# Two sequence mixers in one kernel: the swapped copy of k made by an engine, the skip on TensorE, another load for x, and a new order

## The chip, the cores and the metric

One Trainium2 chip, one core of it. The metric is the device time of one execution in microseconds; less is better. The kernel before has a median of 215.62 us over three runs (215.46 to 218.27).

## The reference

Two mixers over a sequence of 2048 positions and 640 channels are computed and laid side by side. All data is bf16.

```python
# A: a diagonal complex state space model, 640 states
Lam_bar = exp(dt * Lam);  B_bar = ((Lam_bar - 1) / Lam)[:, None] * Bmat
h[t] = Lam_bar * h[t-1] + B_bar @ x[t]
a = 2 * Re(h @ Cmat.T) + x * Dskip
# B: a long convolution with two gates
kv = shift4(k, shift_k) * v          # a causal filter of 4 taps in each channel
y  = irfft(rfft(pad(kv)) * rfft(pad(ssm_k)))[:2048] + kv * ssm_D
b  = q * y
out = concatenate([a, b], axis=-1)   # 2048 x 1280
```

## The kernel before, in words

Everything is straight-line code. A plan lists some 500 items (`make_plan`), each with a name, the engine, its dependencies and a function; the string `ORDER` lists the names in the order in which they are recorded, so each engine's own order is that order restricted to its items. `@2` gives the PSUM pair that an item uses (four pairs, @0 to @6), and `!` picks the other engine for items that name one (an evacuation goes to VectorE instead of ScalarE). Instructions on one engine run in that order; waits between engines come from the data.

Mixer A treats the sequence in four phases s (position modulo 4), 512 positions each, and five blocks j of 128 states. x of phase s, channels on the partitions, is `xT{s}`: for the phases in `NAT` it is loaded naturally (`load_xn`), transposed by TensorE (`xt`) and copied out of PSUM (`xe`); for the others it is loaded by a transposing DMA on SyncE's queue (`load_xt`). Item `v{s}_{j}` (TensorE, `pe_in`) multiplies B and x, and for s other than 1 adds the previous phase times Lambda; `ve{s}_{j}` evacuates. The order in a block is s = 1, 2, 3, 0: phase 0 then holds four steps in one, and a scan over 512 positions is done on it: a rotation with a cosine and sine table (`tabs`, from POOL's phases `tp{j}` and ScalarE's `tab{j}`), the scan and the rotation back (`rs{j}`, `rout{j}`). `od{s}_{j}` makes the other phases from it on VectorE, and `p{i}_{s}` (TensorE, `pe_proj`) projects 128 positions of a phase onto the 640 outputs: 20 matmuls of 320 columns. The skip x * Dskip is added by six more matmuls with a diagonal matrix, or, for the eight blocks in `SKV`, by VectorE: x rows are loaded (`xs`), multiplied by Dskip (`skip_x`, `xd`) and added while evacuating (`dve_yo`). Otherwise ScalarE evacuates (`act_yo`). `yd{i}_{s}` stores.

Mixer B goes through five groups G of 128 channels. k and v are loaded transposed (`kT`, `vT`). The four taps (`tap{G}_{m}`) are matmuls of 64 x 64 diagonal matrices, two halves of the array at once, and need a second copy of k with its channel halves swapped, `kS`: two DMAs from SBUF to SBUF (`swap_k`). `kv` multiplies by v on VectorE, `kvo` stores kv to a DRAM scratch, `kvs` reads it back as rows, `hs` reads the filter. The transform is done in two steps of matmuls (`s1`, `s2`, h for the filter, k for kv; `he`/`ke` are the evacuations) with tables G and R, `y{G}_{hf}` is the complex product of the spectra on VectorE, `inv` the first inverse step with table H, `zt` a transposing DMA, `fin` the last step, `ob` the gate by q on VectorE, `od_` the store. The tables come from phases on POOL (`gp`, `hp`) through sines on ScalarE (`G`, `H`).

Of the kernel before, what the change touches and what calls it, by code (L numbers as in the profile page):

```python
# [29 lines left out]
SKV = [(i, s) for i in (2, 3) for s in range(4)]  # L30
RAW = (0, 1)
NAT = (1, 2)
# [13 lines left out]
class Kernel:  # L46
# [487 lines left out]
    def rotate(self, out, v, j, back):  # L534
        tt = self.nc.vector.tensor_tensor
        c, s = (self.tabs[:, j, i:i + 1, :].to_broadcast([128, 2, M]) for i in range(2))
        tt(out=self.rot_p, in0=c, in1=v, op=ALU.mult)  # L537
# [67 lines left out]
    def swap_k(self, eng):  # L605
        for h in range(2):
# [3 lines left out]
            eng.dma_start(out=self.kS[64 * h:64 * h + 64], in_=src)  # L610
# [56 lines left out]
    def dve_y(self, hf):  # L667
# [3 lines left out]
        cr = self.rot[:].rearrange("p a n -> p (a n)").rearrange("p (r n) -> p r n", r=2)  # L671
        tt(out=cr, in0=X[:, ::-1, :], in1=self.Hf[:, 1:2, hs].to_broadcast([128, 2, 1024]), op=ALU.mult)  # L672
        tt(out=X, in0=X, in1=self.Hf[:, 0:1, hs].to_broadcast([128, 2, 1024]), op=ALU.mult)  # L673
        for r in range(2):
            tt(out=X[:, r, :], in0=X[:, r, :], in1=cr[:, r, :], op=ALU.add if r else ALU.subtract)  # L675
# [39 lines left out]
def make_plan(K):  # L715
# [48 lines left out]
    for q in range(3):  # L764
        A(f"dL{q}", "DVE", 0.83, ["lam", "dc"], lambda q=q: K.dve_diagL(q))
# [58 lines left out]
    for j in J:  # L824
# [31 lines left out]
    for G in range(NG):  # L856
# [3 lines left out]
        dma(f"kS{G}", "SP", 1.1, 1.1, [f"kT{G}"] + ([f"tap{G - 1}_{m}" for m in range(2)] if pre else []), lambda e, G=G: K.swap_k(e))  # L860
# [51 lines left out]
s1h0_1@4 bg3@0 H2 s1h0_0@6 dS1 v3_0@2 gp2 H3 bge3!@0 s1he0_1@4 s1he0_0!@6 kT1 s1h0_2@0 ve3_0@2 s1h0_3@4 gp3 s1he0_2!@0 s1he0_3@4
nH kvs0 v0_0@6 G2 pow G3 s2h0_3@2 ve0_0!@6 s2h0_2@0 prr s2he0_3@2 s2h0_1@4 kS1 rs0 v1_4@6 s2he0_1@4 vT1 s2he0_2@0 ve1_4@6
s1k0_3@2 s1k0_0@4 s1ke0_3@2 s1k0_1@0 hs1 s1ke0_1!@0 tap1_0@6 s1k0_2@2 s1ke0_0!@4 tap1_1@0 s1ke0_2@2 s2h0_0@4 kv1_0@6 s2k0_1@2
s2he0_0@4 kv1_1@0 v1_2@6 s2ke0_1@2 rout0 kvo1 CT0 s2k0_2@4 ve1_2@6 s2k0_3@0 od2_0 s2k0_0@2 s2ke0_2@4 v1_1@6 s2ke0_3@0 kT2 had1
y0_1 s1h1_2@4 v2_2@0 s1he1_2@4 s2ke0_0@2 kvs1 ve1_1@6 s1h1_0@4 ve2_2@0 y0_0 s1h1_1@2 inv0_2@6 v3_2@0 zs0_2@6 s1he1_1@2 s1he1_0@4
# [92 lines left out]
```

## Time and profile before

| | |
|---|---|
| median of three runs | 215.62 us |
| the profiled execution | 216.61 us, of which the span is 214.8 |
| TensorE (PE) busy | 189.7 us, 88% |
| VectorE (DVE) busy | 187.6 us, 87% |
| ScalarE (ACT) busy | 130.4 us, 61% |
| POOL busy | 40.1 us, 19%, all in the first 44 us |
| DMA queue of SyncE | 86.6% of the 16 DMA engines' span |
| mean granted clock of TensorE | 0.984 |

A timeline row reads: start in us, duration in us, engine, line of the program, operation, output<-input, count, and in brackets the idle time before it and what ended that. A windows row reads: the window and its length, then busy time and number of instructions of PE, PEld (weight loads), DVE, ACT and POOL (or of the one engine or line that the question was confined to), then the granted clock, the DMA share and the GB/s. A group's row reads: line, engine, operation, tiles, shape, count | busy, mean ns | idle time before it.

### The profile page before, as it was taken

To read this page: it belongs to the slowest core of one execution; us is meant where nothing else is said; L and a number is where in the kernel's file an instruction comes from. 1 tells how busy PE (TensorE), PEld (TensorE's weight loads), DVE (VectorE), ACT (ScalarE), POOL (GpSimd) and SP (SyncE) were. 2 spreads that over 40 slices of the span, in tenths; PEclk is the share of its full clock that TensorE was granted. 3 is DMA by queue.
4 is the path that set the end of the run, shared out by engine and by line. 5 is a ranking of instruction groups with operands and counts; after the bars stand their busy time and mean duration, and the time that the engine had idled before them with its cause. 6 is when DMAs were issued, how large, how long until landed. Compare 5 with 4: busy or idle time off the path is not lost.

```text
span 214.8 us, 7500 instructions
## 1 busy us (share of the span) xinstructions
PE 189.7 (88%) x3322; PEld 129.3 (60%) x3322; DVE 187.6 (87%) x304; ACT 130.4 (61%) x145; POOL 40.1 (19%) x73
## 2 busy tenths in 40 slices
PE   0854849898999999899899999997999999999993
PEld 0723715455646647556775455775778787887772
DVE  2799899759999899999999999999999999991472
ACT  2392853877678586997977858785557856010100
POOL 8799999910000000000000000000000000000000
PEclk9998888999999999999999999999999999999999
DMA  6899902999699999899957999899880757888965
GB/s 185 216 248 183 184 5 79 191 174 176 158 219 148 159 194 148 156 168 197 164 142 155 140 198 157 139 242 197 193 139 3 160 165 167 125 205 167 206 199 145
DMA packets 123517, 35.41 MB, mean 165 GB/s; under 512 B 116055, under 2 KB 122844, under 8 KB 123484
## 3 DMA queue, kind: packets, MB, share of 16 engines
q1 hardware_dynamic: 123424, 34.92, 86.6%
q8 instruction: 26, 0.43, 0.9%
q14 instruction: 7, 0.06, 0.1%
q10 hardware_dynamic: 60, 0.01, 0.0%
HBM read 12.30 MB, written 7.86 MB: 94 GB/s over the span
## 4 chain that ended last, share of the span: by engine, by line
PE 51%; DVE 22%; POOL 10%; DMA 8%; ACT 4%; issue 3%; ACTq 1%; SPq 0%; DVEq 0%
PE ps L572 21%; PE ps L523 11%; PE ps L662 4%; DVE vT L638 4%; PE ps L649 4%; DMA zz<-zz 3%; DMA xT<-in_A_x_dram 3%; POOL qb L460 3%; POOL kv_st L460 2%; PE ps L683 2%; DMA As_h<-in_A_Lambda_im_dram 2%; PE ps L702 2%; DVE z L546 2%; DVE rot L537 1%; PE ps L684 1%
## 5 line engine op out<-in xcount | busy, mean ns | idle before, releaser
L523 PE MATMUL ps<-xT,BT 128*128 128x512 bf16 x200 | 51.6, 395 | 4.3 <-ACT xT L470 2.6
L523 PEld LDWEIGHTS <-BT 128*128 128x128 bf16 x200 | 19.1, 100 | 27.3 <-issue 6.1
L572 PE MATMUL ps<-Cs,hs 128*128 128x320 bf16 x240 | 34.9, 299 | 0.0
L572 PEld LDWEIGHTS <-hs 128*128 128x128 bf16 x240 | 22.5, 98 | 8.4
L662 PEld LDWEIGHTS <-G 128*64 128x64 bf16 x640 | 19.3, 109 | 7.3 <-issue 5.9
L470 ACT CAST Hf<-ps 128x1024 bf16<-128x1024 f32 x20 | 19.8, 1025 | 3.0 <-PE ps L662 3.0
L470 ACT CAST As_h<-ps 128x1024 bf16<-128x1024 f32 x17 | 16.7, 1027 | 7.0 <-PE ps L649 4.3
L470 ACT CAST zz<-ps 128x1024 bf16<-128x1024 f32 x15 | 14.6, 1030 | 7.7 <-PE ps L686 7.7
L470 ACT CAST Xs<-ps 128x1024 bf16<-128x1024 f32 x19 | 19.0, 1030 | 0.1
L470 ACT CAST As_kv<-ps 128x1024 bf16<-128x1024 f32 x17 | 16.9, 1027 | 2.9 <-PE ps L649 2.9
L683 PE MATMUL ps<-Xs,H 128*128 128x128 bf16 x80 | 17.6, 220 | 0.3 <-ACT Xs L470 0.2
L686 PE MATMUL ps<-Xs,H 128*128 128x128 bf16 x80 | 17.5, 219 | 0.0
L685 PE MATMUL ps<-Xs,H 128*128 128x128 bf16 x80 | 17.5, 219 | 0.0
L684 PE MATMUL ps<-Xs,H 128*128 128x128 bf16 x80 | 17.5, 219 | 0.0
L594 ACT CAST BT<-ps 128x640 bf16<-128x640 f32 x8 | 5.6, 695 | 18.2 <-PE ps L577 16.2
L633 PE MATMUL ps<-kT,diagS 64*64 64x512 bf16 x80 | 11.1, 397 | 5.1 <-DVE BT L468 2.8
L675 DVE TENSOR_TENSOR Xs<-Xs,rot 128x1024 bf16<-128x1024 bf16 x20 | 12.9, 687 | 0.3
L662 PE MATMUL ps<-As_kv,G 128*64 128x128 bf16 x320 | 11.7, 221 | 1.3 <-ACT As_h L470 1.2
L672 DVE TENSOR_TENSOR rot<-Xs,Hf 128x2048 bf16<-128x2048 bf16 x10 | 12.2, 1224 | 0.7
L662 PE MATMUL ps<-As_h,G 128*64 128x128 bf16 x320 | 12.1, 221 | 0.8 <-ACT zz L470 0.5
L673 DVE TENSOR_TENSOR Xs<-Xs,Hf 128x2048 bf16<-128x2048 bf16 x10 | 12.2, 1225 | 0.6
L470 ACT CAST hs<-ps 128x1024 bf16<-128x1024 f32 x8 | 8.2, 1020 | 6.4 <-PE ps L526 5.2
(201 smaller groups left out, 422.4 us busy)
## 6 DMA issues: line engine op xcount, KB each, us to landing
h_st<-in_B_ssm_k_dram SPq DMA_DIRECT2D x10, 256.0 KB, 5.7
kv_rows<-vT SPq DMA_DIRECT2D x5, 512.0 KB, 3.3
kv_st<-kv_rows SPq DMA_DIRECT2D x10, 256.0 KB, 5.5
qb<-in_B_q_dram SPq DMA_DIRECT2D x5, 512.0 KB, 5.7
out_dram<-qb SPq DMA_DIRECT2D x5, 512.0 KB, 3.9
out_dram<-BT SPq DMA_DIRECT2D x16, 160.0 KB, 2.8
kS<-kT SPq DMA_DIRECT2D x10, 129.0 KB, 3.3
zz<-in_A_x_dram SPq DMA_DIRECT2D x2, 640.0 KB, 4.2
```

The costliest lines, as they stand in the source:

```text
L470: self.nc.scalar.copy(out=out, in_=in_)
L523: mm(o, lhsT=self.BT[:, r, k, j * 128:(j + 1) * 128], rhs=xT[:, k, :], start=(k == 0), stop=(s == 1 and k == NT - 1))
L572: mm(o[:, 0:320], lhsT=h[:, r, ts], rhs=self.Cs[:, r, j, c0:c0 + 320], start=(j == 0 and r == 0), stop=(not on_pe and j == NT - 1 and r == 1))
L633: self.nc.tensor.matmul(ps[cols, r, :], lhsT=self.diagS[rows, 4 * v + j, :], rhs=rhs, start=(j == 0), stop=(j == 3))
L662: self.nc.tensor.matmul(o[64 * e:64 * e + 64, c:c + 128], lhsT=self.G[:, r, k, :], rhs=As[:, k, :], start=True, stop=True)
L672: tt(out=cr, in0=X[:, ::-1, :], in1=self.Hf[:, 1:2, hs].to_broadcast([128, 2, 1024]), op=ALU.mult)
L673: tt(out=X, in0=X, in1=self.Hf[:, 0:1, hs].to_broadcast([128, 2, 1024]), op=ALU.mult)
L675: tt(out=X[:, r, :], in0=X[:, r, :], in1=cr[:, r, :], op=ALU.add if r else ALU.subtract)
L683: mm(o_re, lhsT=self.H[:, 0, k1, :], rhs=yre, start=True, stop=False)
L684: mm(o_re, lhsT=self.H[:, 2, k1, :], rhs=yim, start=False, stop=True)
L685: mm(o_im, lhsT=self.H[:, 1, k1, :], rhs=yre, start=True, stop=False)
L686: mm(o_im, lhsT=self.H[:, 0, k1, :], rhs=yim, start=False, stop=True)
```

## The change

- `swap_k` becomes an item of VectorE, or of ScalarE where the order marks it with `!`: two copies of 64 partitions x 1032 elements from one partition half to the other, in place of the two DMAs. In the new order kS0 stays on VectorE and kS1 to kS4 are marked.
- `SKV` is empty: all sixteen projection blocks add the skip on TensorE and are evacuated by ScalarE. The x rows, their multiplication and their sum on VectorE go.
- `NAT` is (1,): x of phase 2 is loaded by a transposing DMA; its 20 transposes on TensorE and two evacuations go.
- The VectorE items are cut: rs into rs, sc; rout into ra, rout; od into oa, od; y into ya, y. The instructions in them are the same.
- `ORDER` is another.

```diff
-SKV = [(i, s) for i in (2, 3) for s in range(4)]
+SKV = []
-NAT = (1, 2)
+NAT = (1,)
...
-    def swap_k(self, eng):
+    def swap_k(self):
         for h in range(2):
             o = PAD - 4 + 512 * h
             src = self.kT[64 - 64 * h:128 - 64 * h, o:o + 1024 + 516]
             src = bass.AP(src.tensor, src.offset, [list(src.ap[0]), [1024, 2], [1, 516]])
-            eng.dma_start(out=self.kS[64 * h:64 * h + 64], in_=src)
+            if self.alt:
+                self.nc.scalar.copy(out=self.kS[64 * h:64 * h + 64], in_=src)
+            else:
+                self.nc.vector.tensor_copy(out=self.kS[64 * h:64 * h + 64], in_=src)
...
-        A(f"rs{j}", "DVE", 4.3, [f"ve0_{j}", f"tab{j}", "prr"], lambda j=j: K.dve_scan(j))
-        A(f"rout{j}", "DVE", 2.05, [f"rs{j}"], lambda j=j: K.dve_out(j))
+        A(f"rs{j}", "DVE", 2.05, [f"ve0_{j}", f"tab{j}"], lambda j=j: K.dve_rot(j))
+        A(f"sc{j}", "DVE", 2.25, [f"rs{j}", "prr"], lambda j=j: K.dve_scan(j))
+        A(f"ra{j}", "DVE", 1.25, [f"sc{j}"], lambda j=j: K.dve_back(j))
+        A(f"rout{j}", "DVE", 0.8, [f"ra{j}"], lambda j=j: K.dve_out(j))
         for s in (1, 2, 3):
-            A(f"od{s}_{j}", "DVE", 2.26, [f"rout{j}", "pow"], lambda j=j, s=s: K.dve_next(j, s))
+            A(f"oa{s}_{j}", "DVE", 0.9, [f"rout{j}", "pow"], lambda j=j, s=s: K.dve_mul(j, s))
+            A(f"od{s}_{j}", "DVE", 1.36, [f"oa{s}_{j}"], lambda j=j, s=s: K.dve_next(j, s))
...
-        dma(f"kS{G}", "SP", 1.1, 1.1, [f"kT{G}"] + ([f"tap{G - 1}_{m}" for m in range(2)] if pre else []), lambda e, G=G: K.swap_k(e))
+        A(f"kS{G}", "DVE", 0.7, [f"kT{G}"] + ([f"tap{G - 1}_{m}" for m in range(2)] if pre else []), lambda: K.swap_k(), alt=("ACT", 2.0))
...
         for hf in range(2):
-            A(f"y{G}_{hf}", "DVE", 3.73, [f"s2ke{G}_{q}" for q in (2 * hf, 2 * hf + 1)] + [f"s2he{G}_{q}" for q in (2 * hf, 2 * hf + 1)],
-              lambda hf=hf: K.dve_y(hf))
+            A(f"ya{G}_{hf}", "DVE", 2.4, [f"s2ke{G}_{q}" for q in (2 * hf, 2 * hf + 1)] + [f"s2he{G}_{q}" for q in (2 * hf, 2 * hf + 1)],
+              lambda hf=hf: K.dve_ym(hf))
+            A(f"y{G}_{hf}", "DVE", 1.33, [f"ya{G}_{hf}"], lambda hf=hf: K.dve_y(hf))
...
-x1 pc lv2 lv0 B0 lv3 pc2 dc3 lsk lv4 dc lv1 pg dc2 gp1 zer kT0 tv@0 pc3 tsk@2 tve@0 B4 exp gp0 B3 rho Fi bt0@4 rr x2 B1 tske@2
+x1 pc lv1 lv4 B1 lv0 pc2 dc lv2 zer lv3 B0 lsk pc3 dc3 kT0 dsel pg pk dc2 gp1 tv@0 tsk@2 tve@0 den exp gp0 rho bt1@4 tske@2 rr
...
```

What the new order moves is seen in the instructions. SyncE's queue in the start, before: from the natural load of x2 (into zz) to the second k.

```order
L179 DMA zz_162<-in_A_x_dram 128x4x640
L176 DMA As_kv_160<-in_A_B_re_dram 128x640
L176 DMA As_kv_160<-in_A_B_im_dram 128x640
L603 DMA_TRANSPOSE vT_155<-in_B_v_dram 128x2048
L610 DMA kS_154<-kT_153 64x2x516 x2
L614 DMA h_st_156<-in_B_ssm_k_dram 64x32x64 x2
L176 DMA As_kv_160<-in_A_B_re_dram 128x640
L176 DMA As_kv_160<-in_A_B_im_dram 128x640
L182 DMA_TRANSPOSE xT3_138<-in_A_x_dram 128x5x512
L641 DMA kv_rows_63<-vT_155 128x2048
L182 DMA_TRANSPOSE xT0_135<-in_A_x_dram 128x5x512
L603 DMA_TRANSPOSE kT_153<-in_B_k_dram 128x2048
```

The same queue after, from the first x by transposing DMA to the first store of kv.

```order
L182 DMA_TRANSPOSE xT2_137<-in_A_x_dram 128x5x512
L182 DMA_TRANSPOSE xT3_138<-in_A_x_dram 128x5x512
L630 DMA h_st_156<-in_B_ssm_k_dram 64x32x64 x2
L182 DMA_TRANSPOSE xT0_135<-in_A_x_dram 128x5x512
L616 DMA_TRANSPOSE vT_155<-in_B_v_dram 128x2048
L176 DMA As_kv_160<-in_A_B_re_dram 128x640
L176 DMA As_kv_160<-in_A_B_im_dram 128x640
L616 DMA_TRANSPOSE kT_153<-in_B_k_dram 128x2048
L176 DMA Xs_139<-in_A_B_re_dram 128x640
L176 DMA Xs_139<-in_A_B_im_dram 128x640
L657 DMA kv_rows_63<-vT_155 128x2048
```

x0 stood behind the store of kv (kv_rows) and now stands four transfers ahead of v and before that store; the transfers of kS are gone.

ScalarE after the change, around the evacuation of v0_0 into z0 (ve0_0), which the first scan reads; H are the tables of the inverse step, BT the scaled B, kS the copy of k.

```order
L470 CAST hs0_140<-ps1_65 128x1024
L463 ACTIVATE tabs_129<-kv_st_157 128x1024
L463 ACTIVATE tabs_129<-qb_158 128x1024
L318 ACTIVATE H_128<-kv_st_157 128x2x512
L318 ACTIVATE H_128<-qb_158 128x2x512
L470 CAST h31_143<-ps2_66 128x2x512
L318 ACTIVATE H_128<-kv_st_157 128x2x512
L470 CAST z0_150<-ps1_65 128x1024
L470 CAST BT_130<-ps3_67 128x2x4x128
L624 COPY kS_154<-kT_153 64x1032 x2
```

Before, VectorE made this evacuation; now it stands on ScalarE behind three of the four H tables, and the copy of k follows two places behind it.

VectorE from the last product of the spectra (Xs) to the end, before: BT holds the output rows, qb the gate.

```order
L675 TENSOR_TENSOR Xs_139<-Xs_139,rot_152 128x1024 x2
L587 TENSOR_TENSOR BT_130<-BT_130 128x640 x2
L591 TENSOR_TENSOR BT_130<-ps3_67,BT_130 128x640
L591 TENSOR_TENSOR BT_130<-ps2_66,BT_130 128x640
L707 TENSOR_TENSOR qb_158<-ps0_64,qb_158 128x16x64
L707 TENSOR_TENSOR qb_158<-ps3_67,qb_158 128x16x64
L468 CAST zz_162<-ps2_66 128x8x32x4
L468 CAST zz_162<-ps0_64 128x8x32x4
L468 CAST zz_162<-ps1_65 128x8x32x4
L587 TENSOR_TENSOR BT_130<-BT_130 128x640
L591 TENSOR_TENSOR BT_130<-ps3_67,BT_130 128x640
L587 TENSOR_TENSOR BT_130<-BT_130 128x640 x2
```

And after, to the end of its list:

```order
L696 TENSOR_TENSOR Xs_139<-Xs_139,rot_152 128x1024 x2
L468 CAST zz_162<-ps1_65 128x8x32x4
L468 CAST zz_162<-ps3_67 128x8x32x4
L728 TENSOR_TENSOR qb_158<-ps1_65,qb_158 128x16x64
L728 TENSOR_TENSOR qb_158<-ps2_66,qb_158 128x16x64
L728 TENSOR_TENSOR qb_158<-ps0_64,qb_158 128x16x64
L728 TENSOR_TENSOR qb_158<-ps3_67,qb_158 128x16x64
```

The multiplications and sums of the skip are gone from it; two casts and four gates are left.

More of the change, by code (lines that the diff above doesn't have):

```diff
@@ L532, in zt, with turn_v @@
         return self.__dict__[f"z{j % NZ}"][:]
[L534 removed]
+    def turn_v(self, v, j):
         tt = self.nc.vector.tensor_tensor
@@ L912 @@
[L912 to L915, printed above, removed]
@@ L938 @@
-yo3_1@4 xs3_3 yd2_1 yd3_0 yd3_1 fin4_1@0 yo2_3@6 fin4_0@2 p3_3@4 xs3_2 ob4_1@0 yd2_3 ob4_0@2 xd3_3 p3_2@6 od_4 xd3_2 yo3_3@4
-yd3_3 yo3_2@6 yd3_2
+x1 pc lv1 lv4 B1 lv0 pc2 dc lv2 zer lv3 B0 lsk pc3 dc3 kT0 dsel pg pk dc2 gp1 tv@0 tsk@2 tve@0 den exp gp0 rho bt1@4 tske@2 rr
+B4 Fi bt0@6 pp x2 be0@6 xt1_1@0 dS0 prr xt1_0@2 G1 pF kS0 tp0 xe1_1!@0 tap0_0@6 trig1 xe1_0@2 lam tap0_1@0 x3 gp3 dL0 tab0
+v1_0@2 be1@4 dL2 G0 tp1 v1_1@4 dL1 ve1_0@2 G3 tp2 hs0 dD v2_0@2 tab1 gam x0 ve1_1@4 tp3 tab2 dS1 v2_1@4 aRM ve2_0@2 tp4 drhs dRM
@@ new lines @@
+tab3 dG vT0 v3_0@2 hp0 tab4 ve2_1!@4 hp1 H0 v3_1@4 ve3_0!@2 B2 hp2 H1 kT1 v0_0@2 ve3_1@4 kv0_0@6 pow H2 kv0_1@0 B3 dcm@4 bg0@6
+ve0_0@2 hp3 dcol@4 kvo0 had0 CT0 v0_1@0 bge0@6 rs0 kS1! gp2 sc0 bg2@4 H3 bg3@2 ve0_1@0 bg1@6 bge3@2 ra0 s1h0_2@0 CT1 G2 v1_2@2
+rout0 bge1@6 nH s1he0_2@0 rs1 v1_3@6 ve1_2@2 ca0 sc1 v2_2@0 kvs0 ve1_3@6 vT1 bge2@4 oa3_0 cs0 s1h0_3@2 ve2_2@0 v1_4@6 s1he0_3@2
+od3_0 ca1 s1h0_0@4 ra1 s1h0_1@0 v2_3@2 s1he0_0@4 rout1 s1he0_1@0 cs1 ve1_4@6 s2h0_2@4 ve2_3@2 oa2_0 s2h0_1@0 qi0 v3_2@6 hs1
```

90 lines of the change are left out of this document (51 added, 39 removed).

## The prediction

> **What bounds the kernel now.** I read the page's busy times first, then the windows by stage, then the rows at the two ends of VectorE's long stretch, then the waits of the DMA queue.
>
> ```profile
> span 214.8 us, 7500 instructions
> PE 189.7 (88%) x3322; PEld 129.3 (60%) x3322; DVE 187.6 (87%) x304; ACT 130.4 (61%) x145; POOL 40.1 (19%) x73
> PE   0854849898999999899899999997999999999993
> DVE  2799899759999899999999999999999999991472
> ```
>
> PE and VectorE are both near 88%, but not in the same place. VectorE's low digits are at the start (slices of 5.4 us) and in the last four slices, where PE still reads 9. So there are three stages: a start, a middle that VectorE fills, and an end that PE fills. Their borders are single rows:
>
> ```profile
> 45.95 1.23 DVE L468 CAST z<-ps 128x1024 bf16<-128x1024 f32 x1 [2.34 <-PE ps L526]
> 47.21 0.69 DVE L537 TENSOR_TENSOR rot<-tabs,z 128x1024 bf16<-128x1024 bf16 x1
> 183.52 1.29 DVE L675 TENSOR_TENSOR Xs<-Xs,rot 128x1024 bf16<-128x1024 bf16 x2
> 211.36 0.82 DVE L591 TENSOR_TENSOR BT<-ps,BT 128x640 bf16<-128x640 f32 x1 [1.25 <-PE ps L572]
> 47.20:184.80 137.60, 131.87 (x2651) 88.65 (x2646) 133.59 (x200) 101.63 (x111) 0.00 (x0) 1.00 0.92 163
> 184.80:214.80 30.00, 26.52 (x288) 20.48 (x285) 17.32 (x23) 1.70 (x2) 0.00 (x0) 1.00 0.78 180
> ```
>
> The first turn of the scan (rs0) begins at 47.2; the last product of the convolution (y4_1) ends at 184.8. In between VectorE (the third busy figure) works 133.6 of 137.6 us; the rest is mostly the small gap between dependent instructions. After 184.8 PE has 26.5 us of work in 30.0 and VectorE 17.3. So the time is 47.2 + 137.6 + 30.0 = 214.8, and a change pays if it starts rs0 earlier, takes work from VectorE between these two points, or shortens the end. VectorE work saved in the last 30 us or before 47.2 pays nothing by itself.
>
> **Why rs0 starts at 47.2.** It needs ve0_0, which needs v0_0, which needs the transposed x0:
>
> ```profile
> 21.00 4.35 SPq L182 DMA_TRANSPOSE xT<-in_A_x_dram  x1
> 35.48 0.34 SPq L641 DMA_DIRECT2D kv_rows<-vT  x1
> 35.87 3.18 SPq L182 DMA_TRANSPOSE xT<-in_A_x_dram  x1
> SPq L641 <- DVE h_st L617: 10.3, 1, 10.3
> SPq L603 <- DMA zz<-in_A_x_dram: 2.7, 1, 2.7
> 42.71 1.25 PE L523 MATMUL ps<-xT,BT 128*128 128x512 bf16 x5 [0.73 <-DMA xT<-in_A_x_dram]
> 45.84 1.53 PE L662 MATMUL ps<-As_h,G 128*64 128x128 bf16 x48
> ```
>
> SyncE's queue is in order (and, as the L603 row shows, a transfer can wait for one issued three places earlier to land). The x0 load stands behind the store of kv (L641), which waits 10.3 us for VectorE; x0 is issued at 35.9 and its product starts at 42.7, 6.8 us later. This product (14 matmuls) takes 45.84 - 42.71 = 3.1 us.
>
> **The start after the change.** In the new order x2, x3 and x0 are three transposes in a row, ahead of vT0 and of the kv store, so the 10.3 us wait no longer stands before x0. With the observed issue times (4.35 each, from about 10) and such waits for the transfer three places ahead, x0 is issued at about 21 and lands at about 28. It isn't what is late next; two chains are, and I follow both.
>
> ```profile
> 10.87 1.20 ACT L470 COPY BT<-ps 128x1280 bf16<-128x1280 bf16 x1
> 9.04 1.28 ACT L373 ACT_TABLE_LOAD   x1
> 21.88 1.04 ACT L301 ACTIVATE G<-Hf 128x1024 bf16<-128x1024 int32 x1
> 24.45 1.42 ACT L470 COPY xT<-ps 128x1536 bf16<-128x1536 bf16 x1
> 13.47 3.87 PE L523 MATMUL ps<-xT,BT 128*128 128x512 bf16 x10 [2.61 <-ACT xT L470]
> 9.97 0.20 POOL L455 TENSOR_TENSOR Fi<-Fi,c 128x5 int32<-128x5 int32 x1 [1.20 <-DVE Fi L366]
> 6.61 2.16 POOL L297 TENSOR_TENSOR Hf<-Hf,gs 128x512 int32<-128x512 int32 x2
> 18.45 2.43 POOL L460 TENSOR_TENSOR qb<-Xs,Fi 128x512 int32<-128x512 int32 x2
> 25.42 3.06 POOL L313 TENSOR_TENSOR kv_st<-kk,bb 128x512 int32<-128x512 int32 x2
> 31.03 2.08 POOL L313 TENSOR_TENSOR kv_st<-kk,bb 128x512 int32<-128x512 int32 x2
> ```
>
> PE's chain: ScalarE now does, from about 10.0, be0 1.2, table load 1.3, one G 1.05, the small sines 0.7, and then the x1 copy 1.4: v1_0 can start at 15.6 (13.5 before). Then 3.9 (cold, as this row), v1_1 2.2 (10 matmuls where 14 take 3.1), and five products of 14 matmuls (v2_0, v2_1, v3_0, v3_1, v0_0) at 3.1 = 15.5: 37.2, plus the copy of v0_0 1.0 = 38.2. POOL's chain: the phases of the tables follow Fi and two G phases, so tp0 starts at about 14.2; tp0 2.1, one G phase 2.8, tp1 to tp4 9.0, three H phases of 2.08 to 3.06, 7.7 together, end at 35.8; on ScalarE H2 (1.05) stands ahead of ve0_0 (1.0): 37.9. The chains agree; with 0.8 for hand-overs I take 39 for rs0. Low bound 36.5, if the matmuls run warm and nothing is handed over late; high bound 47.2, as now.
>
> The Trainium skill, "TensorE: Matmul & The Clock Gate", Part 1, says the array runs at half clock until some 3.4 us of sustained activity, and that an idle stretch of that length cools it again. The 3.87 us row (2.2 warm) fits, after 2.6 us of idleness. By the rule the new order, which has both tap groups on PE just before v1_0, would find it warm: PE's chain ends 1.7 us earlier; the POOL chain still holds rs0 at about 38, so the sum by the rule is about 1 us lower.
>
> **The middle after the change.** rs, sc, ra, rout and oa, od, ya, y are the same instructions as before under new names; splitting an item adds none. Between rs0 and y4_1 VectorE has, before, these evacuations and skip multiplies among the rest:
>
> ```profile
> 47.20:184.80 137.60, 9.65 (x8) 1.00 0.92 163
> L587 DVE TENSOR_TENSOR BT<-BT 128x640 bf16<-128x640 bf16 x2 | 1.0, 482 | 0.0
> L322 DVE TENSOR_SCALAR H<-H 128x2048 bf16<-128x2048 bf16 x1 | 0.7, 684 | 0.0
> ```
>
> (The first row is L468 alone.) After: seven casts instead of eight (-1.2), no skip multiply (one lies inside, about -0.5), and nH has moved inside (+0.7): -1.0, so 136.6. The large saving on VectorE, eight adds of 0.82 and eight multiplies of 0.48, lies almost all in the last 30 us and pays nothing there beyond what PE allows. kS0 is the only copy of k that stays on VectorE, in the start; kS1 to kS4 carry the mark for ScalarE.
>
> ```profile
> kS<-kT SPq DMA_DIRECT2D x10, 129.0 KB, 3.3
> L470 ACT COPY xT<-ps 128x1024 bf16<-128x1024 bf16 x1 | 1.0, 1022 | 0.0
> L468 DVE COPY xT<-ps 128x1024 bf16<-128x1024 bf16 x1 | 0.7, 673 | 0.0
> L594 ACT CAST BT<-ps 128x640 bf16<-128x640 f32 x8 | 5.6, 695 | 18.2 <-PE ps L577 16.2
> ```
>
> One kS is two copies of 64 x 1032: by the nearest rows 1.35 on VectorE and 2.05 on ScalarE, so 8.2 us more on ScalarE, against transfers of 3.3 us that no engine computed. Neither is on the chain alone: kv1 to kv4 are wanted many microseconds after kT lands. But ScalarE's load in the middle goes from 101.6 us to about 124: counted in the new order between bge0 and the last evacuation before y4_1, 106 casts at 1.03 = 109, four kS = 8.2, seven output copies at 0.70 = 4.9, Cs and G 4.4, less some handed over at the borders. That is 88% of the stretch instead of 74%, with four PSUM pairs between PE and those who empty them, so VectorE will wait more often for a result. Bounds for this wait: zero, since 16 us of ScalarE remain free, and 22, if every added microsecond came through. I take 5, near the low end, because most of VectorE's middle items work in SBUF on data already there; at the first places where it is close (rs2 behind v0_2, y1, y2) I count 1 to 2 us each. Middle: 136.6 + 5 = 141.6.
>
> **The end after the change.** Behind y4_1 PE has two inverse groups, one fin, seven projection blocks and two fins; before, more of the blocks were left, but without the skip.
>
> ```profile
> 166.08 1.53 PE L572 MATMUL ps<-Cs,hs 128*128 128x320 bf16 x10
> 169.18 0.45 PE L649 MATMUL ps<-R,kv_st 64*64 64x64 bf16 x32
> 180.98 5.60 PE L572 MATMUL ps<-Cs,hs 128*128 128x320 bf16 x40
> 186.42 0.63 PE L702 MATMUL ps<-Mq,zz 128*128 128x64 bf16 x16
> 186.88 0.22 PE L683 MATMUL ps<-Xs,H 128*128 128x128 bf16 x1
> 187.78 0.63 PE L702 MATMUL ps<-Mq,zz 128*128 128x64 bf16 x16
> ```
>
> A block with the skip on PE takes 3.0 (166.08 to 169.18, less the small gap), without it 2.72 (half of 180.98 to 186.42): 0.3 a block, 2.4 us for the eight. A fin takes 0.46 (186.42 to 186.88), the 16 inverse matmuls behind it 0.9 (to 187.78). So 2 x 0.9 + 3 x 0.46 + 7 x 3.0 = 24.2, the last copy on ScalarE 0.7, and from there to the end 2.6 as now (212.2 to 214.8): 27.5. The twenty fewer PE transposes of x2 lie in the start, off the chain.
>
> **Sum.** 39.0 + 141.6 + 27.5 = 208.1 of span. The profiled execution took 216.61 with 214.8 inside; the median of the runs, 215.62, is 0.8 above that span. So 208.9 us, 3.1% less.
>
> **Rivals.** (1) The start gains little: three transposed x loads in a row, where two were, share the queue with kT0 and h, and ve0_0 sits behind table work on ScalarE. If each x landed 6.8 us after the one before, x0 is there at about 31 and nothing changes; but if POOL's or ScalarE's queue slips by 6 us, rs0 starts at 45, and 45 + 141.6 + 27.5 + 0.8 = 214.9: no change. For it: ScalarE has 16 items of tables and copies before ve0_0; against it: the wait of 10.3 is really gone. (2) ScalarE takes VectorE's place as the bound of the middle. Place: the kS copies and evacuations in one in-order queue, with a PSUM pair held for each; price: all 22 us come through, 39 + 136.6 + 22.4 + 27.5 + 0.8 = 226.3, slower by 5%. It decides the sign from about 12 us of wait on (then 215.9), and 16 us make it slower by over 2%. For it: 88%; against it: the page's ScalarE waits are for PE, and VectorE has a queue of ready work. (3) The order does better than I count: no wait in the middle and warm matmuls, 37 + 136.6 + 27.5 + 0.8 = 201.9.
>
> Beside the first rival: the Trainium skill, "VectorE: DVE Perf Modes", Rules for kernel authors, tells to transpose 128 x 128 blocks on TensorE where PSUM will do, and by DMA otherwise; for x2 the change goes the other way. No run here shows x2 both ways; by the rule it would be the late start, 214.9.
>
> **How the numbers follow.** The forecast has 0.52 (204 to 212.5), the late start 0.20, ScalarE as the bound 0.16 (half of it beyond 2%), the better order 0.12. The bounds of the start (36.5 to 47.2) and of the waits (0 to 22) give 202 to 227; leaving out a tenth on either side: 202.5 to 218. A measurement of this kernel tells about 2% from no change, so faster means below 211.3 and slower above 219.9: faster 0.62 (nearly all of the forecast and the better order), same 0.25, slower 0.13.
>
> **What would show it.** rs0's first multiply at 37 to 41; x0 issued before the first kv store; VectorE busy about 133 us between it and the last Xs subtraction, with under 8 us of waits; ScalarE near 124 there; PE without idle time in the last 25 us, and VectorE almost idle there. The prediction is wrong if rs0 starts after 44, or if VectorE's idle time before casts, rotations or products, released by ScalarE or PE, is over 10 us.

## The result, and the profile after

The changed kernel takes 214.85 us (median of 20 runs), the kernel before in the same comparison 216.12: ratio 0.993, 95% interval 0.9902 to 0.9958. That is 0.7% less; 208.9 us, 3.1% less, had been predicted. A few executions of every kernel run longer at a lower granted clock: they are in the medians below but not in the ratios. The profiled execution took 213.54 us, with a span of 211.8; it is the shortest of the 20, and the profiled one before (216.61) is longer than its median, so the two spans lie 3.0 us apart where the medians lie 1.3 apart. From its page:

```profile
span 211.8 us, 7505 instructions
PE 185.3 (88%) x3337; PEld 129.8 (61%) x3350; DVE 175.2 (83%) x282; ACT 148.8 (70%) x167; POOL 40.5 (19%) x73
PE   0789960999999999989988999988989799999993
DVE  3789999649999999999999999999999889950040
PEclk9999996799999999999999999999999999999998
```

VectorE lost 12 us of work, but the span only 3. PE's line has a hole in the sixth and seventh slice (from about 30 to 37 us) that it did not have before, and the granted clock falls behind it. VectorE's next low digits are in the eighth and ninth slice (37 to 47.7 us); the first rotation begins only at 45.9. The borders of the three stages, from VectorE's timeline:

```profile
45.89 0.69 DVE L537 TENSOR_TENSOR rot<-tabs,z 128x1024 bf16<-128x1024 bf16 x1 [0.31 <-ACT z L470]
182.15 1.29 DVE L696 TENSOR_TENSOR Xs<-Xs,rot 128x1024 bf16<-128x1024 bf16 x2
```

And the same two windows as before:

```profile
45.90:183.40 137.50, 129.94 (x2880) 93.81 (x2890) 132.76 (x199) 119.41 (x130) 0.00 (x0) 1.00 0.87 153
183.40:211.80 28.40, 24.67 (x274) 19.07 (x270) 7.12 (x7) 5.88 (x9) 0.00 (x0) 0.98 0.65 142
```

| | before | predicted | after |
|---|---|---|---|
| start, until rs0 | 47.2 | 39.0 | 45.9 |
| middle, rs0 to the last Xs subtraction | 137.6 | 141.6 | 137.5 |
| end | 30.0 | 27.5 | 28.4 |
| span | 214.8 | 208.1 | 211.8 |

The start is 6.9 us later than predicted, the middle 4.1 shorter, the end 0.9 longer. PE's timeline names what is late in the start:

```profile
15.74 5.56 PE L523 MATMUL ps<-xT,BT 128*128 128x512 bf16 x24 [0.83 <-ACT xT L470]
37.31 2.29 PE L523 MATMUL ps<-xT,BT 128*128 128x512 bf16 x5 [7.22 <-DVE hs L468]
41.62 1.24 PE L523 MATMUL ps<-xT,BT 128*128 128x512 bf16 x5
```

PE waits 7.2 us before v3_1, for VectorE's cast of v2_1 (item ve2_1, into hs). What this cast reads was complete: the matmuls of v2_1 ended at 26.9. VectorE's own queue shows where it stood (not all of its rows):

```profile
16.09 4.70 DVE L386 TENSOR_TENSOR diagL<-ident,lamb 128x640 bf16<-128x640 bf16 x3
...
23.40 0.89 DVE L425 TENSOR_TENSOR pq<-nn,vec 128x10 f32<-128x10 f32 x1
...
25.41 0.90 DVE L429 TENSOR_TENSOR gam<-pq,rden 128x10 f32<-128x10 f32 x1
26.34 0.97 DVE L430 TENSOR_SCALAR gam<-gam 128x10 f32<-128x10 f32 x1
...
31.99 1.01 DVE L284 TENSOR_TENSOR Mq<-m_cv,m_mask 128x64 bf16<-128x64 f32 x1
32.93 3.19 DVE L386 TENSOR_TENSOR H<-ident,gamb 128x384 bf16<-128x384 bf16 x3
36.05 1.21 DVE L468 CAST hs<-ps 128x1024 bf16<-128x1024 f32 x1
```

The cast is behind the set-up of tables (gam, R, the diagonals), and this set-up is slow: an operation on ten numbers a partition takes 0.9 us. Two queues the prediction did follow went as it said. From SyncE's queue: x0, issued at 19.82 (about 21 predicted), stands behind h and directly ahead of v, far ahead of the first store of kv (40.68), and it does not gate.

```profile
9.71 7.13 SPq L182 DMA_TRANSPOSE xT<-in_A_x_dram  x2
19.82 4.32 SPq L182 DMA_TRANSPOSE xT<-in_A_x_dram  x1
40.68 0.33 SPq L657 DMA_DIRECT2D kv_rows<-vT  x1
```

POOL's phases run without a gap, and the third H phase ends at 35.2 (35.8 predicted):

```profile
18.49 3.20 POOL L460 TENSOR_TENSOR kv_st<-Xs,Fi 128x512 int32<-128x512 int32 x2
24.23 2.05 POOL L460 TENSOR_TENSOR kv_st<-Xs,Fi 128x512 int32<-128x512 int32 x2
32.88 2.35 POOL L313 TENSOR_TENSOR kv_st<-kk,bb 128x512 int32<-128x512 int32 x2
```

So the theory: the start is set by a third chain, VectorE's in-order queue, in which two evacuations stand behind a set-up that is stretched because POOL works beside it. The experiments test both halves of this.

### The profile page after: what moved, and what is told of

It is laid out like the page before. It is cut to its first block, busy times and chain, and to the rows that moved or that the text cites. A ratio compares the mean times of both kernels' runs of the same rounds, so it can differ in the third digit from the quotient of the medians.

```text
span 211.8 us, 7505 instructions
## 1 busy us (share of the span) xinstructions
PE 185.3 (88%) x3337; PEld 129.8 (61%) x3350; DVE 175.2 (83%) x282; ACT 148.8 (70%) x167; POOL 40.5 (19%) x73
## 4 chain that ended last, share of the span: by engine, by line
PE 31%; DVE 13%; ACT 6%; issue 2%; DVEq 0%; ACTq 0%
PE ps L585 18%; PE ps L678 3%; DVE qb L728 2%; PE ps L590 2%; PE ps L723 2%; DVE Xs L696 2%; ACT Xs L470 1%; PE ps L704 1%; ACT As_kv L470 1%; DVE Xs L691 1%; ACT BT L607 1%; DVE rot L690 1%; PE ps L707 1%; PE ps L706 1%; PE ps L705 1%
## 5 line engine op out<-in xcount | busy, mean ns | idle before, releaser
L523 PE MATMUL ps<-xT,BT 128*128 128x512 bf16 x189 | 48.6, 386 | 9.3 <-DVE hs L468 7.2
L585 PE MATMUL ps<-Cs,hs 128*128 128x320 bf16 x240 | 36.3, 299 | 0.6 <-ACT Hf L470 0.5
L607 ACT CAST BT<-ps 128x640 bf16<-128x640 f32 x16 | 11.1, 692 | 24.7 <-PE ps L590 18.3
L585 PEld LDWEIGHTS <-hs 128*128 128x128 bf16 x240 | 22.0, 98 | 8.4 <-issue 0.5
L728 DVE TENSOR_TENSOR qb<-ps,qb 128x1024 bf16<-128x1024 f32 x10 | 11.8, 1217 | 14.2 <-ACT BT L607 14.1
L470 ACT CAST As_kv<-ps 128x1024 bf16<-128x1024 f32 x20 | 19.5, 1036 | 0.0
L470 ACT CAST zz<-ps 128x1024 bf16<-128x1024 f32 x16 | 15.9, 1027 | 5.0 <-PE ps L707 4.9
L470 ACT CAST As_h<-ps 128x1024 bf16<-128x1024 f32 x19 | 18.7, 1031 | 0.8 <-PE ps L665 0.8
L470 ACT CAST Hf<-ps 128x1024 bf16<-128x1024 f32 x17 | 17.3, 1031 | 0.1
L585 PE MATMUL ps<-Cs,h 128*128 128x320 bf16 x80 | 12.1, 299 | 0.0
```

Source lines behind the costliest of these rows:

```text
L470: self.nc.scalar.copy(out=out, in_=in_)
L523: mm(o, lhsT=self.BT[:, r, k, j * 128:(j + 1) * 128], rhs=xT[:, k, :], start=(k == 0), stop=(s == 1 and k == NT - 1))
L585: mm(o[:, 0:320], lhsT=h[:, r, ts], rhs=self.Cs[:, r, j, c0:c0 + 320], start=(j == 0 and r == 0), stop=(not on_pe and j == NT - 1 and r == 1))
L728: self.nc.vector.tensor_tensor(out=self.qb[:, :, cs].rearrange("p a (i c) -> p a i c", c=4), in0=ps[:].rearrange("p a n -> p (a n)").rearr ...
```

## The experiments

All in one table; the start, the middle and the end are those of one profiled execution each, cut at the same two rows as above; the ratio is to the kernel before, run beside it, with its 95% interval.

| kernel | median us | ratio | start | middle | end |
|---|---|---|---|---|---|
| the change | 214.85 | 0.993 (0.9902 to 0.9958) | 45.9 | 137.5 | 28.4 |
| early casts on ScalarE | 210.59 | 0.975 (0.9686 to 0.9815) | 39.05 | 140.6 | 28.3 |
| early casts first in VectorE's queue | 211.15 | 0.976 (0.9704 to 0.9816) | 41.2 | 139.95 | 28.35 |
| less POOL work (one run) | 204.26 | | 36.4 | 137.7 | 28.4 |
| x2 natural | 212.37 | 0.9813 (0.976 to 0.9866) | 41.8 | 139.9 | 28.4 |
| kS by transfers | 212.89 | 0.9858 (0.9811 to 0.9905) | 41.4 | 140.7 | 28.5 |
| before, skip on PE | 218.68 | 1.0112 (1.0056 to 1.0168) | 47.0 | 137.5 | 32.4 |
| before, x0 early | 214.9 | 0.9948 (0.992 to 0.9976) | 46.4 | 137.9 | 30.0 |
| early and late casts on ScalarE | 214.62 | 0.9892 (0.9836 to 0.9948) | 39.06 | 146.0 | 28.1 |
| early casts on ScalarE, kS1 to kS4 by transfers | 210.66 | 0.9723 (0.9678 to 0.9768) | 39.06 | 141.1 | 28.6 |
| the same, late casts on ScalarE | 215.28 | 0.9926 (0.9894 to 0.9959) | 39.05 | 144.4 | 28.05 |
| early casts on ScalarE, all kS by transfers | 212.13 | 0.9775 (0.9723 to 0.9826) | 41.6 | 141.3 | 28.2 |
| before, x2 by a transposing load | 217.31 | 1.0018 (0.9981 to 1.0054) | 46.4 | 139.6 | 30.0 |

### The two early casts

On ScalarE (a `!` in the order means VectorE for these items):

```diff
-ve2_1!@4
+ve2_1@4
-ve3_0!@2
+ve3_0@2
```

> The changed kernel with one thing undone in the start: the evacuations ve2_1 and ve3_0 of the first value block (two casts of 128x512 out of PSUM) go to ScalarE, which is idle there for 7.8 us, and no longer to VectorE. Theory A (these two casts stand in VectorE's own in-order queue behind diagL, diagD, the ten small operations of gam, dS1, drhs, dRM and dG; PE waits 7.2 us for ve2_1 and rs0, the first rotation, comes as late as that makes it): PE's 7.2 us wait for ve2_1 falls below 1.5 us, v3_1 starts at 30 to 33 instead of 37.3, rs0 starts at 39 to 41 instead of 45.9, the middle stays at 137 to 139 and the end at 28 to 29: total 5 to 7 us shorter than the changed kernel, 208 to 210 us, ratio to the kernel before 0.965 to 0.975. Rival B (the POOL chain of the rotation tables or the transposing loads of x set the start, as the prediction had it among its own chains): the wait moves to another name and rs0 stays at 44 to 46: ratio 0.99 to 1.00. Rival C (the start comes earlier, the middle gives it back as VectorE then waits for ScalarE or PE): rs0 at 40, the middle 4 us or more longer, ratio above 0.985.

On PE's timeline of this kernel, then on ScalarE's and VectorE's:

```profile
30.37 1.24 PE L523 MATMUL ps<-xT,BT 128*128 128x512 bf16 x5 [0.24 <-ACT hs L470]
```

```profile
36.62 1.01 ACT L470 CAST z<-ps 128x1024 bf16<-128x1024 f32 x1 [0.24 <-PE ps L526]
36.10 2.34 DVE L654 TENSOR_TENSOR vT<-ps,vT 128x1024 bf16<-128x1024 f32 x2
38.71 0.53 DVE L633 TENSOR_TENSOR h_st<-h_st,dcol_b 128x32 bf16<-128x32 bf16 x1
39.05 1.57 DVE L537 TENSOR_TENSOR rot<-tabs,z 128x1024 bf16<-128x1024 bf16 x1
40.55 0.68 DVE L538 TENSOR_TENSOR rot<-tabs,z 128x1024 bf16<-128x1024 bf16 x1
41.26 2.33 DVE L542 TENSOR_TENSOR rot<-rot 128x512 bf16<-128x512 bf16 x2
```

The wait of 7.2 is gone, v3_1 starts at 30.4, and rs0 at 39.05, the place that the prediction gave it. But it isn't the prediction's chains that hold it there: z, which rs0 reads, was complete at 37.6, and VectorE, without a gap since 14.4, came to rs0 only 1.4 us later, behind the product with v (vT) and two small items. Its own queue still sets the start. Theory A holds for the start; the ratio is at the upper end of what it expected (4.3 us shorter than the change by the medians, not 5 to 7), because the middle is 3.1 us longer, not 0 to 1.5. Most of that is in the rows of rs0: it now runs while POOL still works (until 43.3), and takes 1.57 and 2.33 us where it took 0.69 and 0.76. This version beats both kernels, with two marks of the order changed.

The same without another engine, by order alone: ve2_1 moved to directly behind v2_1, and dS1, dRM and dG moved behind it.

```diff
-dS1 v2_1@4
+v2_1@4 ve2_1!@4 dS1
-ve3_0!@2
+ve3_0!@2 dRM
-kv0_1@0
+kv0_1@0 dG
```

(dRM and dG are taken from their old places ahead of vT0.)

> The changed kernel with the two casts ve2_1 and ve3_0 left on VectorE and only its order changed: ve2_1 directly behind the call of v2_1, ahead of dS1; dRM (three tables) behind ve3_0; dG (three tables) behind kv0_1. No operation is added, removed or moved to another engine. Theory A (place in VectorE's queue): ve2_1 runs at about 28.5 instead of 36.05, PE's wait for it falls from 7.2 to under 2 us, but dRM and dG, 6.3 us together, are still ahead of rs0 on VectorE: rs0 at 41 to 44, total 2 to 5 us shorter than the changed kernel, ratio to the kernel before 0.972 to 0.985. Rival B (another chain is the gate): rs0 at 45 to 46, ratio 0.99 to 1.00.

VectorE's timeline of this kernel:

```profile
28.30 1.21 DVE L468 CAST hs<-ps 128x1024 bf16<-128x1024 f32 x1
41.20 0.70 DVE L537 TENSOR_TENSOR rot<-tabs,z 128x1024 bf16<-128x1024 bf16 x1
```

Theory A: ve2_1 runs at 28.3 instead of 36.05, rs0 at 41.2, ratio 0.976. The place in the queue alone gives back 4.7 us of the start; the other engine gives 2.2 more, of which the total shows nothing (0.975 beside 0.976).

### Is the set-up slow because of POOL?

```diff
-        for r in range(2):
+        for r in range(2 if j == 0 else 0):
```

(in `pool_tab`; the same in `pool_H` with q, and the sines read the first buffer.)

> The changed kernel without the GpSimd phases of the tables tp1 to tp4 and hp1 to hp3 (their sines are taken of the first table's phases again, so the output is another one); everything else, order included, is the same. Question: are VectorE's operations of 10 to 36 us long because GpSimd works beside them? Theory A (they are: both engines hold each other up): the small operations of gam, 0.89 to 1.00 us each beside GpSimd, fall to 0.15 to 0.25, diagL and dG lose a third or more, VectorE's set-up ends by 30 instead of 36, the wait of PE for ve2_1 falls under 2 us and rs0 comes at 38 to 41. Rival B (they are long by themselves or for lack of their inputs): the durations stay within 10% and rs0 at 45 to 46.

VectorE's timeline of this kernel:

```profile
22.62 0.17 DVE L425 TENSOR_TENSOR pq<-nn,vec 128x10 f32<-128x10 f32 x1
23.21 0.17 DVE L429 TENSOR_TENSOR gam<-pq,rden 128x10 f32<-128x10 f32 x1
25.11 2.33 DVE L386 TENSOR_TENSOR H<-ident,gamb 128x384 bf16<-128x384 bf16 x3
27.37 1.21 DVE L468 CAST hs<-ps 128x1024 bf16<-128x1024 f32 x1
```

Theory A: the same instructions take 0.17 instead of 0.9, and from the first of gam (22.3) to the cast of v2_1 it is 5.0 us instead of 13.8: 8.7 us of VectorE's queue were time that POOL's work cost it. rs0 comes at 36.4, earlier than the 38 to 41 expected. diagL did not shorten (4.70): POOL is still at work beside it, until 21.7. dG (H) fell from 3.19 to 2.33, by 27%, not by a third. The cast out of PSUM takes 1.21 with POOL and without.

In the kernel before, gam ran at 15 us, when POOL had only short operations; there it was as quick. VectorE and POOL before:

```profile
15.15 0.17 DVE L425 TENSOR_TENSOR pq<-nn,vec 128x10 f32<-128x10 f32 x1
```

```profile
15.17 0.23 POOL L270 TENSOR_TENSOR m_ph<-m_ph,m_t 128x16 int32<-128x16 int32 x1
```

So the order moved nine tiny operations from a place where they cost 0.17 each to one where most cost 0.9.

The Trainium skill, "SBUF — State Buffer", Who interferes with whom, says that VectorE and GpSimd share one pair of ports under an exclusive lock, held for the whole instruction; its section "SBUF: two separate sides" counts on VectorE's side operations with two SBUF inputs or in a two-port mode. These rows agree for the products with two inputs and for the casts out of PSUM, which were not touched. A one-input operation on ten f32 numbers (L430) was held too, 0.97 instead of 0.17; whether it ran in such a mode no run here shows.

### Two parts undone, and the same surprise twice

x2 natural again: its load, its 20 transposes (xt2) and two evacuations (xe2) behind ve1_0.

```diff
-NAT = (1,)
+NAT = (1, 2)
-ve1_0@2
+ve1_0@2 xt2_0@2 xe2_0@2 xt2_1@2 xe2_1@2
```

> The changed kernel with two of the four x loads natural instead of one: x2 too is loaded row by row and turned by TensorE (four more calls, xt2 and xe2, behind ve1_0). Theory A (x lands in time and the late casts on VectorE set rs0): rs0 at 45 to 47, total within 1 us of the changed kernel. Rival B (the transposing loads still make the start late): the products of v2 and v3 start earlier, rs0 by 3 us or more, total 3 us or more shorter.

kS by transfers again, as in the kernel before:

```diff
-            if self.alt:
-                self.nc.scalar.copy(out=self.kS[64 * h:64 * h + 64], in_=src)
-            else:
-                self.nc.vector.tensor_copy(out=self.kS[64 * h:64 * h + 64], in_=src)
+            eng.dma_start(out=self.kS[64 * h:64 * h + 64], in_=src)
```

> The changed kernel with one part undone: the swapped copy of k comes by transfers from kT again, in the same places of the order, so VectorE loses 0.88 us near 12 us and ScalarE loses four copies of 2.1 us in the middle; SyncE's queue gets ten transfers more. Theory A (none of the copies is on the path that sets the end: VectorE waits for the cosine at 13.7 to 14.4 anyway, and ScalarE is not the bound of the middle): rs0 at 45 to 46.5, middle 137 to 138, total within 1 us of the changed kernel, ratio to the kernel before 0.988 to 0.998. Rival B (ScalarE's load counts in the middle): the middle gets 2 us or more shorter, ratio under 0.985. Rival C (the transfers of k were worth replacing: they hold up x0 or kT in SyncE's queue): rs0 or a later product later by 2 us or more, ratio above 1.00.

Both start the scan earlier than the change, and in no way that was expected: rs0 is at 41.8 and 41.4, though products of v start later, not earlier (with x2 natural v2_0 starts at 24.1, when the change is already at v2_1; with kS by transfers already v1_0 is late, at 19.8 instead of 15.7, as the taps wait for kS). The first is clearly faster than the change (0.9813 beside 0.993); the interval of the second just touches that of the change. The timelines of the kernel with kS by transfers, POOL's first, then VectorE's and PE's:

```profile
21.24 2.62 POOL L460 TENSOR_TENSOR qb<-Xs,Fi 128x512 int32<-128x512 int32 x2
25.58 2.04 POOL L460 TENSOR_TENSOR kv_st<-Xs,Fi 128x512 int32<-128x512 int32 x2 [1.72 <-ACT tabs L463]
```

```profile
22.99 0.89 DVE L425 TENSOR_TENSOR pq<-nn,vec 128x10 f32<-128x10 f32 x1
24.00 0.17 DVE L427 TENSOR_TENSOR pq<-pq 128x5 f32<-128x5 f32 x1
24.27 0.17 DVE L429 TENSOR_TENSOR gam<-pq,rden 128x10 f32<-128x10 f32 x1
32.83 1.21 DVE L468 CAST hs<-ps 128x1024 bf16<-128x1024 f32 x1
34.09 1.24 PE L523 MATMUL ps<-xT,BT 128*128 128x512 bf16 x5 [0.31 <-DVE hs L468]
```

The late v1 holds up ScalarE's queue (3.9 us before the first cast of hs), ScalarE holds up the tables' buffers, and POOL pauses for 1.72 us. In that pause VectorE's small operations fall from 0.89 to 0.17, with all POOL work still done; the cast of v2_1 comes 3.2 us earlier (32.83 for 36.05) although v1 is 4 us later. PE, which waited 0.3 us and not 7.2, makes the next five matmuls in 1.24 us and not 2.29, which is most of the rest of the 4.5 us. With x2 natural ScalarE waits for PE's transposes of x2 instead; POOL's pause is the same, in nearly the same place:

```profile
26.04 2.04 POOL L460 TENSOR_TENSOR kv_st<-Xs,Fi 128x512 int32<-128x512 int32 x2 [1.71 <-ACT tabs L463]
```

My expectation for both (rs0 at 45 to 47) was wrong, as it took VectorE's durations for fixed. The middle got no shorter without the kS copies (140.7), so rival B of the second falls.

What the first kS copy on VectorE is worth shows only where the early casts are out of the way:

> The kernel of the first experiment with all five copies of k by transfers. It prices the first copy on VectorE in a start where VectorE and PE both have no idle time. With the transfer the tap products waited 3.06 us for kS and the first product of v started at 19.8 instead of 15.7. Theory A (that delay goes through PE's chain, and the pause of GpSimd that came with it pays less here): rs0 at 40.5 to 42.5, total 1.5 to 3.5 us longer than the first experiment, ratio to the kernel before 0.98 to 0.99. Rival B (the pause of GpSimd makes up for it): rs0 at 38 to 40, ratio 0.968 to 0.978.

```diff
-kS0 ... kS1! ... kS2! ... kS3! ... kS4!
+kS0 ... kS1 ... kS2 ... kS3 ... kS4
```

(made on the kernel with the early casts on ScalarE, with the transfers of the edit above). rs0 goes from 39.05 to 41.6, as theory A says. In the start of these two profiled executions the copy by an engine is the better way by some 2.5 us, where in the change, with its late casts, it came out 4.5 us worse. In the total the gain isn't shown: the medians are 1.5 us apart, the ratio of 0.9775 is just under the 0.98 expected, and its interval overlaps that of 0.975.

### The parts alone, on the kernel before

```diff
-SKV = [(i, s) for i in (2, 3) for s in range(4)]
+SKV = []
```

(and the items xs, xd and Db of VectorE's skip taken out of the old order)

> The kernel before with one part of the change alone: all skip blocks on PE (no x blocks loaded again, no multiplication and no sum on VectorE, the outputs evacuated by ScalarE), in the old order. By the prediction's sum each block costs PE 0.3 us more and VectorE loses eight times 1.3 us, almost all of it behind the last product of the convolution, where PE sets the pace. Theory A: rs0 at 47 as before, the middle 0.5 to 1 us shorter, the end 28 to 30.5 (30.0 before): total 0 to 2 us shorter, ratio 0.99 to 1.00. Rival B (VectorE set the end too): the end under 27, ratio under 0.985. Rival C (PE's 2.4 us more come through): the end 31 or more, ratio above 1.005.

The window behind the last Xs subtraction (184.80 to 214.80 with 26.52 of PE before):

```profile
184.54:216.90 32.36, 28.86 (x332) 22.79 (x330) 8.20 (x8) 6.62 (x10) 0.00 (x0) 1.00 0.61 143
```

Rival C: PE's 2.4 us (eight times 0.3) come through whole, and VectorE's 9 us less pay nothing. The skip on PE makes the old order slower by 1.1%. In the new order PE has 24.67 us left in this window instead of 28.86, and the end is 28.4; no run has the new order without the skip on PE.

```diff
-x3 tp4 tab3 dL1
+x3 x0 tp4 tab3 dL1
```

(and x0 taken from its old place behind bg0)

> The kernel before with the transfer of x0 issued directly behind that of x3, ahead of the store of kv that waited 10.3 us for VectorE; nothing else is moved. The prediction read the old start as set by x0 (issued at 35.9, product at 42.7). Theory A (it was only the last of several to be late: PE waited 0.73 us for x0 and was busy until 42.0 in its own order, with v0_0 behind the first step of h): rs0 at 46 to 47.3, total at most 1 us shorter, ratio 0.994 to 1.002. Rival B (the prediction's reading, x0 is the gate): rs0 at 44 or earlier, ratio 0.985 or less.

```profile
46.42 0.69 DVE L537 TENSOR_TENSOR rot<-tabs,z 128x1024 bf16<-128x1024 bf16 x1
```

rs0 at 46.4, ratio 0.9948 (by this 1.1 us shorter, at most 1 was expected): theory A. The row that I had read as the gate (PE waits 0.73 us for x0) was worth 0.8 us of the start. PE had its own order of work up to 42.

> The kernel before with one part of the change alone: x2 loaded by a transposing transfer, its two groups of PE transposes and two copies left out, the rest in the old order. Theory A (x2 lies off the path that sets the old start, PE and VectorE lose 1 to 2 us of work there): rs0 at 46 to 47.5, total within 1.5 us of before, ratio 0.992 to 1.003. Rival B (the third transposing load holds up the queue of SyncE, so kS, v or x0 land later): rs0 at 49 or more, ratio over 1.008. Rival C (the start is bound by PE's work, and twenty transposes less show): rs0 under 45.5, ratio under 0.99.

```diff
-NAT = (1, 2)
+NAT = (1,)
```

(and xt2_0, xt2_1, xe2_0, xe2_1 taken out of the old order.) Ratio 1.0018 (0.9981 to 1.0054): theory A. The start is 0.8 us shorter, the middle 2.0 longer. The Trainium skill, "VectorE: DVE Perf Modes", Rules for kernel authors, prefers TensorE for 128 x 128 transposes; measured alone, the two ways show no difference here (on the new order x2 natural was faster, with POOL's pause in it).

### Is ScalarE a bound of the middle?

Early casts on ScalarE, and every `!` of an evacuation behind rs0 taken away (nine):

```diff
-s2he3_3!@6
+s2he3_3@6
...
```

> The kernel of the first experiment (both early casts on ScalarE) with the nine other evacuations that VectorE keeps, seven of them in the middle and two behind it, moved to ScalarE too; ScalarE then makes every evacuation behind the first rotation. VectorE loses about 7 x 1.2 = 8.4 us in the middle and ScalarE gets 7 x 1.03 = 7.2 us there, to 126 of about 137. Theory A (VectorE is the bound of the middle, ScalarE has room): the middle falls from 140.6 to 132 to 137, total 203 to 207, ratio to the kernel before 0.945 to 0.965. Rival B (ScalarE, at 87% of the middle, takes VectorE's place as the bound, the second rival of the prediction): PE and VectorE wait for ScalarE, the middle stays or grows, total 208 or more, ratio 0.97 or more.

The kernel with only the early casts moved, and kS1 to kS4 by transfers:

```diff
-kS1! ... kS2! ... kS3! ... kS4!
+kS1 ... kS2 ... kS3 ... kS4
```

> The kernel of the first experiment (both early casts on ScalarE) with the four later copies of k (kS1 to kS4) by transfers again and the first one on VectorE as in the change. ScalarE loses 4 x 2.1 = 8.4 us in the middle, from 119 to 111; the start is untouched but for kS1. Theory A (87% is not yet a bound: in the middle the copies of k fill time that ScalarE has): middle 139.5 to 141 (140.6), total within 1 us of the first experiment, ratio to the kernel before 0.970 to 0.980. Rival B (ScalarE's load was felt there too): middle 138.5 or less, ratio under 0.968. Rival C (the transfers hold up SyncE's queue, which is in order, and with it kT, vT or a store): middle 142 or more, ratio over 0.985.

And on top of that the nine marks taken away:

> The kernel of the experiment before this one (copies of k by transfers, 8.4 us less on ScalarE) with the nine late evacuations of VectorE moved to ScalarE, as in the kernel that lost 5.4 us in its middle by that move. ScalarE's middle is then near 118 us, below that of the changed kernel, and VectorE's 8 us shorter. Theory A (that loss came from ScalarE's whole load, 125 us): the middle now falls to 132 to 137, total 200 to 205, ratio 0.935 to 0.955. Rival B (it came from the places: between the fourth and fifth spectrum each moved cast stands in ScalarE's in-order queue behind others and VectorE wants its result at once, whatever the mean load): VectorE still waits 5 us or more for ScalarE behind 150 us, the middle stays at 143 to 146, ratio 0.98 or more.

VectorE's waits between 150 and 186 us in the first of these three kernels, and between 60 and 186 in the last:

```profile
DVE rot L690 <- ACT Xs L470: 5.0, 2, 4.3
DVE rot L690 <- ACT Hf L470: 2.0, 1, 2.0
```

```profile
DVE qb L728 <- PE ps L723: 9.2, 3, 4.3
DVE rot L690 <- ACT Xs L470: 5.2, 2, 4.5
DVE rot L690 <- ACT Hf L470: 2.0, 1, 2.0
```

And that kernel's middle:

```profile
39.05:183.45 144.40, 132.20 (x2896) 94.96 (x2894) 127.45 (x192) 117.65 (x130) 4.09 (x5) 0.99 0.88 162
```

The two kernels with the copies of k by transfers, first with VectorE keeping the nine casts, then without, between 148 and 178 us (VectorE is the third busy figure, ScalarE the fourth):

```profile
148.00:178.00 30.00, 26.76 (x708) 22.70 (x706) 27.52 (x31) 23.30 (x26) 0.00 (x0) 1.00 1.02 169
148.00:178.00 30.00, 24.71 (x671) 20.93 (x669) 15.79 (x20) 28.10 (x31) 0.00 (x0) 0.94 0.84 138
```

Taking 8 us from ScalarE changes nothing (0.9723 beside 0.975), so ScalarE's load over the whole middle is no bound there. Moving the nine casts costs 5.4 us of middle with 125 us on ScalarE and still 3.3 with 118, under the load that it has in the change; theory A of the first and of the last kernel falls. Rival B of the last kernel has its numbers right (the middle of 144.4 and the ratio of 0.9926 are in its range, VectorE waits 7.2 us for ScalarE's spectra behind 150), but it is half of the story. Seven of the nine casts fall into these 30 us. There ScalarE works 28.1 of 30 us with them and 23.3 without, and VectorE falls from 27.5 to 15.8: it waits for the spectra, and about as long for PE's last products (the row of qb, of which 6.7 us lie inside the middle). So it is not ScalarE's sum over the middle, but the sum in this stretch comes close to being a bound; whether another place in ScalarE's queue would help there, no run shows.

## Why the prediction was wrong

**The step that failed is the start.** "PE's chain" and "POOL's chain", with "0.8 for hand-overs", gave 39. Both chains were sized well: PE's v1_0 started at 15.7 (15.6), POOL's third H phase ended at 35.2 (35.8), and with nothing but the two casts moved z is complete at 37.6 (37.9 to 38.2). Missing was a third chain, VectorE's own queue. The prediction looked up each queue that x0 passes, but not the one through which PE's five products in a row had to go: ve2_1 and ve3_0 carry the mark for VectorE, and the set-up ahead of them runs without a gap until 36.0. The cost is 6.9 us in the start. The rival of a late start had the time (rs0 at 45, total 214.9) with another cause: it was neither the loads nor a slip of POOL or ScalarE, and that its total agrees with the 214.85 measured is luck, its middle being 4.1 us too long and its end 0.9 too short. And following this queue would not have been enough. By the durations of the trace of before (0.17 to 0.19 for each of gam's operations, 1.4 us together instead of 5.9) an estimate would have had the set-up end 4.5 us too soon. The durations themselves depended on what POOL did at that moment.

**The old start** was misread: x0's late issue (35.9) was only the last of several things, worth 0.8 us of rs0 and not 8.

**The clock.** v1_0 did run warm: 24 matmuls took 5.56 us together, where my 3.9 us was for ten. After the 7.2 us wait five matmuls took 2.29 us where they take 1.24, and the granted clock was 0.51 between 37 and 40 us. The rule of the Trainium skill ("TensorE: Matmul & The Clock Gate", Part 1), full clock after some 3.4 us of sustained work and half clock after as long an idle stretch, agrees with these two rows. Whether it explains the row of 3.87 us before, as the prediction had it, stays open: the idle time ahead of that row was 2.6 us, and the granted clock in its window (13.4 to 17.4 us) is 1.00.

**The middle**: 136.6 and 5 us of added waits predicted, 137.5 measured; so the term of 5 us came to 0.9 (all of VectorE's waits in this stage to about 2). ScalarE had 119.4 us there, not 124. The rival with ScalarE as the bound does not hold for this order; what it warned of is real for casts in the last stretch. With the early casts on ScalarE the three stages (39.05, 140.6, 28.3) come to 208.0 us, beside the 208.1 predicted. That is luck in two terms: VectorE's queue adds 1.4 us to the start where 0.8 for hand-overs stood, and the 3 us more in the middle are mostly POOL beside rs0, not waits for ScalarE.

**The end**: 28.4 for 27.5. PE's work of 24.67 us was close to the 24.2 predicted, and VectorE was nearly idle (7.1).

**The bounds.** The 202 to 227 do not follow from the two terms: a start of 36.5 with no waits gives 201.4, and 47.2 with 22 us of waits gives 234.1.

**Where the gain of 3 us of span came from**: 1.3 from the start, 1.6 from the end, 0.1 from the middle, in the two profiled executions. Of the parts alone, on the kernel before, the skip costs 1.1% and x2 nothing that shows. That leaves the order and the copies of k, which were not run alone on the kernel before; that the order pays is argued, not shown. Two marks in it gave 1.8% away (0.993 to 0.975).

## What to carry to other kernels

Follow every engine's own queue to the point that sets the stage, not only the transfers and the longest chain: an evacuation on a "busy anyway" engine is only as early as everything ahead of it. Do not carry a duration over to another place in time without asking which engine works beside it there. And when a kernel gets faster because something was delayed, look for the engine that paused.

## What was not expected of the hardware

VectorE operations on SBUF data of 5 to 15 elements a partition took 0.15 to 0.20 us without POOL products beside them and 0.89 to 1.00 beside POOL products of about 1.02 us each; often the next one passed at 0.15. It works both ways: a pair of POOL products took 2.04 us beside the small operations and 3.20 beside diagL. Casts out of PSUM (1.21 to 1.23) and the products with a PSUM input (2.34 for two) were the same in all kernels. So in these kernels small set-up work belongs before or behind the stretch in which POOL has its long products.
